# Reordered loads, four output banks for the first block, and weight sums on GpSimd in a retention-plus-GELU-layer kernel

## The chip, the cores and the metric

The kernel runs on one core of a Trainium2 chip. The metric is the device time of one execution in microseconds (us). The kernel before has a median of 300.85 us over three runs (299.17, 300.85 and 300.95).

## The reference

Eight batches of 576 tokens with eight heads of 64 go through a causal retention (attention without softmax, with a decay per head), and the 4608 x 512 result goes through a two-layer GELU network:

```python
def _attn_ref(q, k, v):
    B, H, S, D_ = q.shape                       # 8, 8, 576, 64
    scores = (1.0 / np.sqrt(D_)) * np.matmul(q, k.transpose(0, 1, 3, 2))
    gamma = 1.0 - 2.0 ** (-5.0 - np.arange(H, dtype=np.float32))
    rel = np.arange(S)[:, None] - np.arange(S)[None, :]
    Dmat = np.where(rel >= 0, gamma[:, None, None] ** rel[None, :, :], 0.0)
    return np.matmul(scores * Dmat[None], v)

def _moe_ref(x, w_in, w_out):                   # x 4608 x 512, w_in 512 x 2048, w_out 2048 x 512
    h = x @ w_in
    g = 0.5 * h * (1.0 + np.tanh(np.sqrt(2.0 / np.pi) * (h + 0.044715 * h * h * h)))
    return g @ w_out
```

## The kernel before

Everything is on one core, with matrix operands in f16 and sums in f32. The output is made in nine blocks t of 512 tokens: block t for t < 8 is the first 512 tokens of batch t, block 8 the 64-token tails of all batches. While TensorE works on the network of block t, it also does the retention of batch t + 1, in small pieces put between the network's matmuls. Every engine runs its instructions in the order in which the program issues them.

**Steps and events.** The main loop at the end (L839 to L869) makes a list of steps for each block and numbers them u = 0, 1, ... After step u it runs what was booked with `at(t, u, ...)`. The list for block 0 is the second layer alone (L841 to L845), because its first layer was done ahead (L833 to L837, with negative u counted back from step 0). For block 0 a step is two matmuls of 512 columns (`down_mm`, L504): for output rows i0 = 0 and 1 sixteen steps, one for each 128-row tile f of w_out in the order `FO` = 0-3, 8-11, 4-7, 12-15, then a step that copies the two PSUM sums out and stores them (`store_pair`, L509); then the same again for rows 2 and 3. So two PSUM banks hold sums at a time, steps 0 to 15 and 17 to 32 are matmuls, and 16 and 33 are stores. Block 1 has sixteen steps of eight 256-column matmuls for its first layer (`up_half`, L480), and after steps 3, 7, 11 and 15 VectorE makes sums of the activations (`act_sums`, L536, four f16 operations each). From step 16 follow fourteen product steps (`prod`, L548): from block 1 on the second layer uses seven products in place of eight, which needs the sums of the activations and the sums `wt` "1" to "4" of w_out's quarters. `weight_sums(f)` (L525) makes the four `wt` sums for half of the rows; they are used in the order "2", "1", "3", "4".

**Retention of one half batch.** `casts2` (L746) books the casts of q and k (GpSimd, with a scale) and of v. `group` (L718) books for 256 tokens: `turn` (L275) for q and k, which is eight transposes on TensorE into one PSUM bank and one copy out (for batch 1 both on ScalarE, for batch 2 the one for q on VectorE); then `first`: `state2`, `score2` (32 matmuls into four banks `st`), the running state (`later`, `scan`, `spread`) and the masks (`masks2`, VectorE, from PSUM); then `second`: `past` and `av2` into two banks `xs`, and two copies `put` on ScalarE into xT, which the next block's first layer reads.

**PSUM.** There are eight banks. `bank` (L61) takes the one at the head of a list, `drop` puts it at the end as soon as its reader is issued in the program. A matmul into a bank waits on the chip until that reader is done.

**Loads.** All loads go through one queue (SyncE, "SP") in the order of `seq` (L124 to L131): batch 0's twelve tiles, sixteen of w_in, sixteen of w_out in the order FO, then batch 1 (`body(1)`, first 256 tokens first), batch 2 and so on. Each is 256 KB into one of sixteen rotating buffers `ld`; each cast frees one, and `pump` (L134) issues the next load. w_out tiles are cast by GpSimd and VectorE in turn (`WENG`, L634).

**Bookings that the change touches** (L711 to L763): the casts of w_out at steps -5 to -2 of block 0, the first half's weight sums on VectorE beside them, the second half's at (0, 28). Batch 1's first group has its casts of q and k at (0, 7), v on ScalarE at (0, 21), turns at (0, 17) and (0, 20), `first` at (0, 23), `second` at (0, 30). Its second group has casts at (0, 14) and (0, 29), turns at (0, 27) and (0, 31), `first` at (1, 1), `second` at (1, 6). Batch 2's two groups follow in block 1. At (1, 16) GpSimd gets a small copy (`gate`, L827) that waits for block 1's last activation sum and holds back the casts of batch 3.

Of the kernel before, what the change touches and what calls it, by code (L numbers as in the profile page):

```python
# [20 lines left out]
def kernel(  # L21
# [9 lines left out]
    nc = tc.nc  # L31
# [87 lines left out]
    def body(b):  # L119
        if b < NPE:  # L120
            return [("b", b, key, 2 * g + y) for g in range(2) for key in "qkv" for y in range(2)]
        return [("b", b, key, c) for c in range(NC) for key in "kqv"]

    seq = body(0) + [("i", g, ct) for g in range(4) for ct in range(4)]  # L124
    FO = [f + g for f in (0, 4) for g in (0, 1, 2, 3, 8, 9, 10, 11)]
    seq += [("o", f) for f in FO]
    TP = {2: 0, 4: 2, 6: 4, 7: 6}
    for b in range(1, B):
        seq += body(b)
        if b - 1 in TP:  # L130
            seq.append(("t", TP[b - 1]))  # L131
    q_ld = {"next": 0, "free": LD, "hold": False}
# [37 lines left out]
    for n in range(2):  # L170
# [3 lines left out]
            out=lp[:, 32 + 16 * n : 48 + 16 * n].rearrange("p (x h) -> p x h", h=8),  # L174
            in0=ps5[:, 4 * n + 2 : 4 * n + 4].unsqueeze(2).to_broadcast([128, 2, 8]),
            in1=lgr.unsqueeze(1).to_broadcast([128, 2, 8]), op=ALU.mult,
# [52 lines left out]
    def new_casts(b):  # L229
        a = att[b]  # L230
        for key in "kqv":
            a[key] = sb.tile([128, W], F16, tag="c" + key, name="c" + key, bufs=1 if key == "q" else 2)
# [38 lines left out]
    def new_turned(b):  # L271
        att[b]["tt"] = t = sb.tile([128, 2, NB, 128], F16, tag="tt", name="tt", bufs=2)
        att[b]["tk"], att[b]["tq"] = t[:, 0], t[:, 1]
# [39 lines left out]
    def score2(b, g, xs=(0, 1)):  # L313
        a = att[b]
        for x in xs:
            st = [bank("st") for _ in range(2)]
            for p in (2 * x, 2 * x + 1):
                for j in range(2):
                    o = 256 * (p % 2) + 128 * j
                    for h, hl in TILES:  # L320
                        nc.tensor.matmul(
                            st[hl][hv(h), o : o + 128], a["tt"][hv(hl), 0, 8 * g + 2 * p + j, hv(h)],
                            tq(b, 2 * g + h, p)[hv(hl)], start=True, stop=True,
                        )
            a["st", g, x] = st

    def masks2(b, g, x):
        for hl, t in enumerate(att[b].pop(("st", g, x))):
            r = sb.tile([128, 512], F16, tag="ret", name="ret", bufs=6)
            nc.vector.tensor_tensor(  # L330
                out=r.rearrange("p (n i) -> p n i", n=2), in0=t.rearrange("p (n i) -> p n i", n=2),
                in1=pm.rearrange("p j i -> p (j i)").unsqueeze(1).to_broadcast([128, 2, 256]), op=ALU.mult,
            )
            drop(t)
            att[b]["ret"][g, hl, x] = r
# [163 lines left out]
    op = {}  # L499
# [9 lines left out]
    def store_pair(t, i0, eng):  # L509
        o = ost()  # L510
        for n in range(2):
            x = op.pop(i0 + n)
            eng[n](out=o[:, n], in_=x)
            drop(x)
        r0 = TB * t + 128 * i0
        nc.sync.dma_start(out=out[r0 : r0 + 256, :].rearrange("(n p) d -> p n d", n=2), in_=o)
# [4 lines left out]
    wt = {n: const.tile([128, NH, HD], F16, name="wt" + n) for n in "1234"}  # L521
    W11, W12 = w_out_sb[:, 0:NH, 0:HD], w_out_sb[:, 0:NH, HD:DM]
    W21, W22 = w_out_sb[:, NH:NF, 0:HD], w_out_sb[:, NH:NF, HD:DM]

    def weight_sums(f, ns=range(4)):  # L525
        s = slice(f, f + 4)
        for n in ns:
            o, x, y, f = (
                ("1", W12, W11, ALU.subtract), ("3", W22, W12, ALU.subtract),
                ("2", wt["3"], W11, ALU.add), ("4", W21, wt["2"], ALU.subtract),  # L530
            )[n]
            nc.vector.tensor_tensor(out=wt[o][:, s], in0=x[:, s], in1=y[:, s], op=f)  # L532

    gs = {}

# [84 lines left out]
    CP = {"i": 0, "o": 0}  # L620

    def cast_w(kind, *i):
        src = w_raw.pop((kind,) + i)
        if kind == "i":
            g, ct = i
            dst = w_in_sb[:, ct, 512 * g : 512 * g + 512]
        else:
            dst = w_out_sb[:, i[0], :]
        eng = WENG[kind][CP[kind] % len(WENG[kind])]
        CP[kind] += 1  # L630
        eng(out=dst, in_=src)  # L631
        pump(1)

    WENG = {  # L634
        "i": (nc.gpsimd.tensor_copy,),
        "o": (nc.gpsimd.tensor_copy, nc.vector.tensor_copy),
    }
# [5 lines left out]
    V, P, A = nc.vector, nc.gpsimd, nc.scalar  # L643


    def later(b, c):
        scan(b, c)
        spread(b, c, A.copy)
# [54 lines left out]
    def at(t, u, f, last=False):  # L703
        events.setdefault((t, u, last), []).append(f)
# [5 lines left out]

    at(0, -12, lambda: [V.memset(x, 0.0) for x in (tbd[1][:, 1:], *tbt[1:])])  # L711
    for n, f in enumerate(FO):
        at(0, -5 + n // 4, lambda f=f: cast_w("o", f))
        if n > 8 and n % 2:
            at(0, -5 + n // 4, lambda n=n: weight_sums(0, [(n - 9) // 2]))


    def group(b, g, turns, s, o, own=True, ahead=()):  # L718
        for w, key, cp in zip(turns, "qk", (A.copy if b == 1 else T, A.copy)):
            at(*w, lambda key=key, cp=cp: turn(b, g, key, (cp,)))  # L720

        def first():
            if own:
                state2(b, g)
            score2(b, g)
            if own:
                later(b, 2 * g)
            masks2(b, g, 0)
            if own:
                masks2(b, g, 1)  # L730
                scan(b, 2 * g + 1)
            else:
                at(s[0], s[1] + 1, lambda: masks2(b, g, 1))

        def second():
            past(b, 2 * g), past(b, 2 * g + 1), av2(b, g)
            for x in ahead:
                state2(*x)
            put(b, 2 * g), put(b, 2 * g + 1)

        at(*s, first)
        at(*o, second)
        if own:
            at(o[0], o[1] + 1, lambda: spread(b, 2 * g + 1, A.copy))

    def casts2(b, g, kq, v, e):  # L746
        at(*kq, lambda: [cc(b, key, 2 * g + y, P) for key in "qk" for y in range(2)])
        at(*v, lambda: [cc(b, "v", 2 * g + y, e) for y in range(2)])

    at(0, 6, lambda: (new_casts(1), new_turned(1)))  # L750
    casts2(1, 0, (0, 7), (0, 21), A)
    group(1, 0, ((0, 17), (0, 20)), (0, 23), (0, 30))
    casts2(1, 1, (0, 14), (0, 29), A)
    at(0, 28, lambda: weight_sums(4))
    group(1, 1, ((0, 27), (0, 31)), (1, 1), (1, 6))
    at(1, 0, lambda: (new_casts(2), new_turned(2)))
    casts2(2, 0, (1, 0), (1, 0), P)
    group(2, 0, ((1, 4), (1, 7)), (1, 11), (1, 16), ahead=((2, 1),))
    casts2(2, 1, (1, 4), (1, 4), P)
    at(1, 17, lambda: later(2, 2))  # L760
    at(1, 23, lambda: later(2, 3))
    group(2, 1, ((1, 10), (1, 13)), (1, 20), (1, 26), own=False)
    at(1, 8, chunk_masks)  # L763

    at(6, 0, lambda: load_tails(TP[7]))
# [38 lines left out]
    for t in range(2, B):  # L804
        b, tl = t + 1, TP.get(t)
# [13 lines left out]
    for b in range(NPE, B):  # L819
        ent = [(key, c) for c in range(NC) for key in "kqv"]  # L820
        eng = {"k": P, "q": P, "v": P if b == NPE else A}
# [17 lines left out]
    for t in range(NTB):  # L839
        steps = []  # L840
        if t == 0:  # L841
            for i0 in (0, 2):
                for f in FO:
                    steps.append(lambda f=f, i0=i0: [down_mm(0, i0 + n, f) for n in range(2)] and None)
                steps.append(lambda i0=i0: store_pair(0, i0, (A.copy, V.tensor_copy)))  # L845
        else:
            for u in range(2 if t == 1 else 0):
                for f in (0, NH, 2, NH + 2, 4, NH + 4, 6, NH + 6):
                    def half(u=u, f=f):
                        up_half(t, u, f)  # L850
                        if f in (NH + 2, NH + 6):
                            return lambda: act_sums(t, f - NH - 2, f - NH + 2, slice(u, u + 1))
                    steps.append(half)
            for f in range(0 if t == 1 else NH):
                steps.append(lambda f=f: up(t, f))
                def hi(f=f):
                    up(t, f + NH)
                    if f % 2:
                        return lambda: act_sums(t, f - 1, f + 1)
                steps.append(hi)  # L860
            for m in (1, 6, 5, 7, 2, 3, 4) if t == NTB - 1 else (1, 6, 5, 7, 2, 4, 3):
                for u in range(2):
                    steps.append(lambda m=m, u=u: (prod(t, m, u), after(t, m, u)))
        for u, s in enumerate(steps):
            then = s()
            run(t, u)
            if callable(then):
                then()
            run(t, u, True)  # L869
# [31 lines left out]
```

## Time and profile before

| what | us |
|---|---|
| median of three runs | 300.85 |
| the profiled execution | 300.83 |
| its span, first to last instruction | 298.9 |
| TensorE busy in the span | 284.7 |
| VectorE, ScalarE, GpSimd busy | 171.9, 163.4, 98.8 |
| TensorE busy in 0 to 20 us | 13.41 of 20.00 |
| in 20 to 34 us (first layer of block 0) | 14.00 of 14.00 |
| in 41.4 to 58 us (block 0's second layer and the start of block 1) | 13.63 of 16.60 |
| in 58 to 89.6 us (rest of block 1) | 31.60 of 31.60 |
| in 89.6 to 268 us (blocks 2 to 7, start of 8) | 178.40 of 178.40 |

The second column is time in the span of one profiled execution; "busy" of TensorE counts matmuls with their modelled ends. The granted TensorE clock is 1.00 in each of these stretches. Block 0's second layer begins at 33.86 us, block 1's first layer at 53.99, its products at 74.04.

### The profile page before, as it was taken

The page shows a single profiled execution, that of the slowest core. Times are in us where ns is not written, and L with a number is a line of the kernel's source. Part 1 is how long each engine was busy: PE and PEld are TensorE (multiplying, and loading weights), DVE is VectorE, ACT ScalarE, POOL GpSimd, SP SyncE. Part 2 cuts the span into 40 slices and gives each one's busy share as a digit, 9 for nine tenths or more (in the row PEclk, how much of TensorE's full clock was granted, in tenths as well). Part 3 has the DMA queues.
Part 4 walks back from the last instruction along what each step waited for, and adds up shares of the span by engine and source line. Part 5 has one row for each costly group of instructions (what it writes and reads, how often), then busy time and mean ns, then how long its engine had stood idle before and what let it go on. Part 6 is the DMA issues. An engine that isn't in the chain of part 4 may idle for free.

```text
span 298.9 us, 7301 instructions
## 1 busy us (share of the span) xinstructions
PE 284.7 (95%) x3028; PEld 197.2 (66%) x3028; DVE 171.9 (58%) x353; ACT 163.4 (55%) x302; POOL 98.8 (33%) x129
## 2 busy tenths in 40 slices
PE   6779988899999999999999999999999999999993
PEld 2458645688884488448844885488548854884582
DVE  6790445998754874476548654855486535233432
ACT  5377426788438673766376736664665356307500
POOL 4677377970790074006700650058030000000000
PEclk9999999999999999999999999999999999999998
DMA  7999999999889999999999959944931030012004
GB/s 200 309 352 350 371 271 293 246 289 211 178 147 230 227 217 183 268 207 195 118 245 227 181 99 263 219 90 86 255 86 37 2 140 0 2 50 94 0 0 140
DMA packets 129057, 52.89 MB, mean 177 GB/s; under 512 B 101633, under 2 KB 120577, under 8 KB 129025
## 3 DMA queue, kind: packets, MB, share of 16 engines
q1 hardware_dynamic: 128544, 51.92, 73.7%
q10 hardware_dynamic: 480, 0.52, 0.6%
q8 instruction: 23, 0.38, 0.5%
q14 instruction: 10, 0.07, 0.1%
HBM read 36.70 MB, written 9.44 MB: 154 GB/s over the span
## 4 chain that ended last, share of the span: by engine, by line
PE 80%; DMA 10%; DVE 4%; SPq 3%; POOL 2%; ACT 1%; issue 0%; DVEq 0%; POOLq 0%
PE hp L469 33%; PE opB L561 14%; PE opA L561 10%; PE opC L561 10%; PE hp L487 4%; DMA ld<-in_moe_w_out_dram 4%; SPq L96 2%; PE xs L448 2%; PE st L372 2%; DMA ld<-in_moe_w_in_dram 2%; DMA ld<-in_q_dram 2%; DMA ld<-in_v_dram 2%; DVE wt L532 2%; PE xs L439 1%; PE us L397 1%; PE tr L285 1%
## 5 line engine op out<-in xcount | busy, mean ns | idle before, releaser
L469 PE MATMUL hp<-xT,w_in_sb 128*128 128x512 f16 x448 | 98.9, 380 | 0.0
L475 ACT ACTIVATE gT<-hp 128x512 f16<-128x512 f32 x112 | 64.9, 597 | 45.3 <-PE hp L469 44.8
L469 PEld LDWEIGHTS <-w_in_sb 128*128 128x128 f16 x448 | 43.3, 98 | 50.6
L561 PEld LDWEIGHTS <-gT 128*128 128x128 f16 x512 | 49.0, 98 | 7.1 <-issue 0.7
L561 PEld LDWEIGHTS <-s 128*128 128x128 f16 x384 | 37.0, 98 | 4.9
L543 DVE TENSOR_TENSOR s<-gT 128x512 f16<-128x512 f16 x32 | 14.0, 436 | 44.4 <-ACT gT L475 44.4
L827 POOL COPY gate<-s 128x1 f16<-128x1 f16 x5 | 0.9, 189 | 92.3 <-DVE s L546 92.3
L561 PE MATMUL opB<-wt,gT 128*128 128x256 f16 x256 | 30.9, 273 | 0.5 <-DVE ost L575 0.5
L487 PE MATMUL hp<-xT,w_in_sb 128*128 128x256 f16 x256 | 30.2, 273 | 1.1 <-POOL w_in_sb L631 1.0
L561 PE MATMUL opA<-w_out_sb,gT 128*128 128x256 f16 x256 | 30.8, 273 | 0.0
L487 PEld LDWEIGHTS <-w_in_sb 128*128 128x128 f16 x256 | 24.4, 98 | 5.1 <-POOL w_in_sb L631 1.6
L423 ACT CAST tbd<-ws 64x256 f16<-64x256 f32 x48 | 19.3, 403 | 15.3 <-DVE ws L414 13.6
L381 DVE TENSOR_TENSOR ret<-st,cm 128x512 f16<-128x512 f32 x40 | 24.8, 681 | 0.0
L575 DVE TENSOR_TENSOR k<-k,opB 128x512 f32<-128x512 f32 x16 | 11.0, 687 | 22.2 <-PE opB L561 16.3
L605 ACT COPY ost<-opA 128x512 f32<-128x512 f32 x8 | 4.7, 586 | 34.2 <-PE opA L561 19.9
L264 POOL TENSOR_TENSOR cq<-ld,sc 128x512 f16<-128x512 f32 x20 | 21.9, 1095 | 0.0
L493 ACT ACTIVATE gT<-hp 128x512 f16<-128x512 f32 x32 | 18.5, 600 | 5.3 <-PE hp L487 5.0
L458 ACT CAST xT<-xs 128x512 f16<-128x512 f32 x36 | 19.3, 592 | 3.3 <-PE xs L362 1.9
L264 POOL TENSOR_TENSOR ck<-ld,sc 128x512 f16<-128x512 f32 x20 | 20.8, 1040 | 0.0
L414 DVE TENSOR_TENSOR ws<-vs,gt 128x256 f32<-128x256 f32 x24 | 16.0, 669 | 1.2
L575 DVE TENSOR_TENSOR ost<-k,opC 128x512 f32<-128x512 f32 x16 | 11.0, 687 | 9.8 <-PE opC L561 9.5
L575 DVE TENSOR_TENSOR ost<-k,opB 128x512 f32<-128x512 f32 (+1 forms) x9 | 5.7, 629 | 18.7 <-PE opB L561 18.7
(93 smaller groups left out, 359.1 us busy)
## 6 DMA issues: line engine op xcount, KB each, us to landing
ld<-in_q_dram SPq DMA_DIRECT2D x32, 256.0 KB, 5.4
ld<-in_k_dram SPq DMA_DIRECT2D x32, 256.0 KB, 5.3
ld<-in_v_dram SPq DMA_DIRECT2D x32, 256.0 KB, 5.3
out_dram<-ost SPq DMA_DIRECT2D x16, 512.0 KB, 3.5
ld<-in_moe_w_in_dram SPq DMA_DIRECT2D x16, 256.0 KB, 6.2
ld<-in_moe_w_out_dram SPq DMA_DIRECT2D x16, 256.0 KB, 6.1
lt<-in_k_dram SPq DMA_DIRECT2D x8, 128.0 KB, 5.1
lt<-in_q_dram SPq DMA_DIRECT2D x8, 128.0 KB, 4.4
```

Source lines behind the costliest of these rows:

```text
L264: eng.tensor_tensor(out=dst.rearrange("p (h d) -> p h d", d=D), in0=raw.rearrange("p (h d) -> p h d", d=D), in1=sc[:, s0].unsqueeze(2).to_ ...
L381: nc.vector.tensor_tensor(out=r.rearrange("p (n i) -> p n i", i=128), in0=t.rearrange("p (n i) -> p n i", i=128), in1=(cm if b < PAIR else ...
L414: nc.vector.tensor_tensor(out=w, in0=uc, in1=gt, op=ALU.mult)
L423: cp(out=(tbd[b % 2][r, c, :, r] if c < NC - 1 else tbt[b % NT4][r, :, r]), in_=w[r])
L458: nc.scalar.copy(out=xT[:, g0 : g0 + 2], in_=xs.rearrange("p (n g t) -> p g n t", n=HP, g=2))
L469: nc.tensor.matmul(hp.rearrange("p (g t) -> p g t", t=TL), w_in_sb[:, ct, 128 * fc : 128 * fc + 128], xT[:, o : o + TB // TL, ct, :], star ...
L475: nc.scalar.activation(out=gT[t][:, fc].rearrange("p i n -> p (i n)"), in_=hp, func=AF.Gelu_apprx_tanh)
L487: nc.tensor.matmul(hp[:, 256 * x : 256 * x + 256].rearrange("p (g t) -> p g t", t=TL), w_in_sb[:, ct, 128 * (f + x) : 128 * (f + x) + 128] ...
L493: nc.scalar.activation(out=gT[t][:, f : f + 2, 2 * u : 2 * u + 2, :].rearrange("p f i n -> p f (i n)"), in_=hp.rearrange("p (f n) -> p f n ...
L543: nc.vector.tensor_tensor(out=s["1"], in0=a21, in1=a22, op=ALU.add)
L561: nc.tensor.matmul(op[tag][:, HD * u : HD * u + HD], lhs(f), rhs[:, f], start=(new and u == 0 and f == 0), stop=(f == NH - 1), skip_group_ ...
L575: nc.vector.tensor_tensor(out=o, in0=a, in1=b, op=ALU.add)
```

## The change

- The load order puts batch 1's first six tiles (q, k, v of its first 256 tokens) ahead of the last four w_out tiles (rows f = 12 to 15).
- These four tiles are cast by GpSimd alone, at (0, 6). Batch 1's q and k are cast at (0, 2), its v at (0, 18).
- Block 0's second layer runs over four banks: twelve steps for rows 0 and 1, twelve for rows 2 and 3, then the last four f for rows 0 and 1 and their store (step 28), then the last four for rows 2 and 3 and their store (step 33).
- Since four banks hold sums, batch 1's first `score2` is split: two banks at `first` (0, 20), the other two four steps later (0, 24).
- The other bookings of batches 1 and 2 move: by one to four steps, the turns of batch 1's second group four and three steps later, to (0, 31) and (1, 0).
- The first half's weight sums stay on VectorE, a step earlier; the second half's move from VectorE at (0, 28) to GpSimd at (1, 5), in the order "3", "2", "1", "4".

```diff
     FO = [f + g for f in (0, 4) for g in (0, 1, 2, 3, 8, 9, 10, 11)]
-    seq += [("o", f) for f in FO]
+    LATE = 12
+    seq += [("o", f) for f in FO[:LATE]]
     TP = {2: 0, 4: 2, 6: 4, 7: 6}
+    seq += body(1)[:6] + [("o", f) for f in FO[LATE:]] + body(1)[6:]
     for b in range(1, B):
-        seq += body(b)
+        seq += body(b) if b > 1 else []
...
-    def weight_sums(f, ns=range(4)):
+    def weight_sums(f, ns, eng):
...
-            nc.vector.tensor_tensor(out=wt[o][:, s], in0=x[:, s], in1=y[:, s], op=f)
+            eng.tensor_tensor(out=wt[o][:, s], in0=x[:, s], in1=y[:, s], op=f)
...
-        eng = WENG[kind][CP[kind] % len(WENG[kind])]
+        eng = WENG[kind][CP[kind] % len(WENG[kind])] if CP[kind] < LATE or kind == "i" else nc.gpsimd.tensor_copy
...
-        at(0, -5 + n // 4, lambda f=f: cast_w("o", f))
-        if n > 8 and n % 2:
-            at(0, -5 + n // 4, lambda n=n: weight_sums(0, [(n - 9) // 2]))
-
-
-    def group(b, g, turns, s, o, own=True, ahead=()):
+        at(0, -5 + n // 4 if n < LATE else 6, lambda f=f: cast_w("o", f))
+        if 8 <= n < LATE:
+            at(0, -5 + n // 4, lambda n=n: weight_sums(0, [n - 8], V))
+
+    def group(b, g, turns, s, o, own=True, ahead=(), apart=0):
...
-            score2(b, g)
+            score2(b, g, (0,) if apart else (0, 1))
             if own:
                 later(b, 2 * g)
             masks2(b, g, 0)
+            if own and not apart:
+                masks2(b, g, 1)
             if own:
-                masks2(b, g, 1)
                 scan(b, 2 * g + 1)
-            else:
+            if apart:
+                at(s[0], s[1] + apart, lambda: (score2(b, g, (1,)), masks2(b, g, 1)))
+            elif not own:
                 at(s[0], s[1] + 1, lambda: masks2(b, g, 1))
...
-    at(0, 6, lambda: (new_casts(1), new_turned(1)))
-    casts2(1, 0, (0, 7), (0, 21), A)
-    group(1, 0, ((0, 17), (0, 20)), (0, 23), (0, 30))
-    casts2(1, 1, (0, 14), (0, 29), A)
-    at(0, 28, lambda: weight_sums(4))
-    group(1, 1, ((0, 27), (0, 31)), (1, 1), (1, 6))
+    at(0, -1, lambda: (new_casts(1), new_turned(1)))
+    casts2(1, 0, (0, 2), (0, 18), A)
+    group(1, 0, ((0, 13), (0, 17)), (0, 20), (0, 29), apart=4)
+    casts2(1, 1, (0, 14), (0, 30), A)
+    group(1, 1, ((0, 31), (1, 0)), (1, 1), (1, 5))
     at(1, 0, lambda: (new_casts(2), new_turned(2)))
     casts2(2, 0, (1, 0), (1, 0), P)
-    group(2, 0, ((1, 4), (1, 7)), (1, 11), (1, 16), ahead=((2, 1),))
+    group(2, 0, ((1, 4), (1, 6)), (1, 10), (1, 15), ahead=((2, 1),))
     casts2(2, 1, (1, 4), (1, 4), P)
-    at(1, 17, lambda: later(2, 2))
+    at(1, 5, lambda: weight_sums(4, (1, 2, 0, 3), P))
+    at(1, 16, lambda: later(2, 2))
     at(1, 23, lambda: later(2, 3))
-    group(2, 1, ((1, 10), (1, 13)), (1, 20), (1, 26), own=False)
+    group(2, 1, ((1, 9), (1, 12)), (1, 20), (1, 26), own=False)
...
-            for i0 in (0, 2):
-                for f in FO:
+            for i0, fs in ((0, FO[:LATE]), (2, FO[:LATE]), (0, FO[LATE:]), (2, FO[LATE:])):
+                for f in fs:
                     steps.append(lambda f=f, i0=i0: [down_mm(0, i0 + n, f) for n in range(2)] and None)
-                steps.append(lambda i0=i0: store_pair(0, i0, (A.copy, V.tensor_copy)))
+                if fs[-1] == FO[-1]:
+                    steps.append(lambda i0=i0: store_pair(0, i0, (A.copy, V.tensor_copy)))
```

## The prediction

> **What bounds the kernel now.** I read the page's busy shares first, then each engine's timeline from 30 to 110 us.
>
> ```profile
> span 298.9 us, 7301 instructions
> PE 284.7 (95%) x3028; PEld 197.2 (66%) x3028; DVE 171.9 (58%) x353; ACT 163.4 (55%) x302; POOL 98.8 (33%) x129
> ```
>
> TensorE is the bound: 14.2 us of the span are idle. From 20 us on it idles in one stretch only, 41.4 to 58 us, where 13.63 of 16.60 us are busy. No matmul is removed, and loads and casts up to the twelfth w_out tile stay as they are, so nothing before step 0 of block 0 (33.86 us) moves. TensorE's timeline there:
>
> ```profile
> 42.39 0.62 PE L285 MATMUL tr<-ident,cq 128*128 128x128 f16 x8 [1.02 <-POOL cq L256]
> 44.40 0.62 PE L285 MATMUL tr<-ident,ck 128*128 128x128 f16 x8
> 46.76 0.19 PE L348 MATMUL us<-cv,ck 64*64 64x64 f16 x1 [0.45 <-ACT cv L251]
> 47.28 0.44 PE L348 MATMUL us<-cv,ck 64*64 64x64 f16 x31 [0.33 <-ACT cv L251]
> 57.62 0.41 PE L321 MATMUL st<-tt 64*64 64x128 f16 x15 [1.07 <-DVE ost L513]
> 57.96 2.79 PE L487 MATMUL hp<-xT,w_in_sb 128*128 128x256 f16 x24
> ```
>
> A row's length holds the drain of its last matmul, so I count starts. A 512-column matmul takes 0.216 us (40 in 8.63 in the chain of waits), a block-0 step 0.432, an `up_half` 0.875, a turn 0.45. From 33.86 to 57.96 the work is 64 x 0.216 + 4 x 0.45 + two states 0.54 + two scores 1.14 + past and av2 0.89 + two up_halves 1.75 = 19.9 us of 24.1. Of the 4.2 lost, the wait for q is 1.2, for k 0.3, for v's casts 1.1, for the copy `ost` (behind VectorE's weight sums) 1.2, and small gaps 0.4. That is all the change could win.
>
> **Part by part: loads and block 0.** The thirteenth w_out tile lands by 37.2 (its GpSimd cast starts at 37.29); q now has its place. Four casts at 1.0 each end q at 39.2 and k at 41.3. TensorE needs q after 28 matmuls, at 39.90, and k at 42.08. Cover 0.7 us; without it the wait is what is missing. So 1.2 + 0.3 are won. The late w_out tiles take the places of k and v, issued from 36.4 to about 40 with 5.2 to 6.1 us to landing; cast by 46.3, the last is needed at step 27, 48.4: no cost. Their two casts more on GpSimd (1.3 us) delay q of the second group to 48.3, needed at 51.0. The store moved behind two loads on SP has a buffer that nobody needs before block 1's products.
>
> The wait for v stays: turn, copy of k and v casts follow each other on ScalarE with three steps of cover, as before. There it was 2.88 us from the turn of k to the state (44.40 to 47.28); here 42.08 + 2.88 = 44.96, again 1.1 lost. From there: rest of state and half a score 0.53, four steps, half a score 0.28, four steps, past and av2 0.89 end `second` at 50.1. Splitting the score costs no matmul; its masks (0.62 each) end by 49.7, needed at 49.85.
>
> A new wait comes next. ScalarE's list before:
>
> ```profile
> 50.49 1.32 ACT L291 COPY tt<-tr 128x1024 f16<-128x1024 f16 x1 [1.32 <-PE tr L285]
> 51.83 1.14 ACT L251 CAST cv<-ld 128x512 f16<-128x512 f32 x2
> 52.88 1.06 ACT L458 CAST xT<-xs 128x512 f16<-128x512 f32 x2
> 53.83 0.82 ACT L423 CAST tbd<-ws 64x256 f16<-64x256 f32 x2
> 54.67 1.01 ACT L291 COPY tt<-tr 128x1024 f16<-128x1024 f16 x1
> 55.58 0.59 ACT L513 COPY ost<-op 128x512 f32<-128x512 f32 x1
> 56.06 1.11 ACT L493 ACTIVATE gT<-hp 128x512 f16<-128x512 f32 x2
> ```
>
> Before, q's copy and v's casts came ahead of the two `put` copies. Now all of it follows them: put 0.95, spread 0.84, v 1.05, q 1.34, ost 0.48, a GELU 0.51, k 1.01 = 6.2 us by start to start, so the second score waits until 50.1 + 6.3 = 56.4. TensorE has 3 steps, 2 turns, 2 up_halves and a state = 4.2 us of cover and arrives at 54.3: 2.1 lost. The `ost` wait goes (VectorE is free). After that score TensorE stands at 57.0 instead of 57.96: **0.95 us won** so far, 299.9.
>
> **Weight sums on GpSimd.** VectorE loses four operations (5.0 us between 51.92 and 56.96); GpSimd gets four of 128x1024 f16, which the trace shows on VectorE only. Nearest rows: GpSimd's two-input operation on 512 columns, 1.04, so 2.05 for 1024; its cast, 0.61, so 1.2 below; and that operation beside VectorE's sums, 2.89 for two, so 2.9 above. I take 2.05, the same kind of operation. [...]
>
> What matters is what VectorE does meanwhile. The timelines of GpSimd and, in the second fence, of VectorE:
>
> ```profile
> 62.15 1.61 POOL L253 CAST cv<-ld 128x512 f16<-128x512 f32 x2
> ...
> 106.97 1.04 POOL L264 TENSOR_TENSOR ck<-ld,sc 128x512 f16<-128x512 f32 x1
> 107.98 1.22 POOL L264 TENSOR_TENSOR cq<-ld,sc 128x512 f16<-128x512 f32 x1
> ```
>
> ```profile
> 62.45 0.83 DVE L543 TENSOR_TENSOR s<-gT 128x512 f16<-128x512 f16 x1
> 63.32 0.71 DVE L544 TENSOR_TENSOR s<-s,gT 128x512 f16<-128x512 f16 x1
> 63.95 0.41 DVE L545 TENSOR_TENSOR gT<-gT 128x512 f16<-128x512 f16 x1
> ...
> 107.07 1.23 DVE L414 TENSOR_TENSOR ws<-vs,gt 128x256 f32<-128x256 f32 x1
> ```
>
> A VectorE operation with two SBUF inputs that starts during a GpSimd operation ends 0.28 us after it: 107.07 + 1.23 = 108.30, GpSimd's at 108.01; the same at 76.80 and 84.87. The activation sums take 0.42 alone, 0.83 and 0.71 beside two casts. GpSimd's next operation is 0.18 longer. Operations with one input in PSUM (masks, copies) keep their length. So the two engines take turns, one operation each. [...]
>
> GpSimd's casts of batch 2 start when q's buffer is free, after the second group's turn of q: 51.6. Eight at 1.01, four at 0.59 and five of 0.18 end at 62.9. The sums then run to 62.9 + 4 x 2.23 = 71.8. VectorE comes to the activation sums after step 7 at 65.0 (GELU done), which are four dependent two-input operations: one gets through after each GpSimd sum, the last at 72.1, where before they took 1.5 us. Behind them on VectorE stands the copy of batch 2's turned q (1.31, before 68.50 to 69.81): 73.4. Who waits: the turn's bank went back to the end of the list, step 10, the state and `score2` take the other seven, so step 11's `hp` gets it. Up to there TensorE has, from 57.0, nine up_halves (steps 2 to 10, 7.9), three turns (1.35), past and av2 (1.11, from 62.79 to 63.90 before) and state and score (0.83) = 11.1, so it arrives at 68.1. It stands until 73.4: **5.3 us lost**. Behind it the masks end at 76.1, needed at 78.8; the remaining sums run alone (GpSimd done by 73.3) before the products at about 79. The `wt` sums are ready in time, and GpSimd is back before its gate.
>
> Sum: 300.83 - 0.95 + 5.3 = **305.2 us**, against 300.83 for the profiled execution (span 298.9 and 1.9 around it), which is the median to 0.02.
>
> **Rivals.**
> - Not slower: the turns on SBUF don't hold VectorE up. Place: activation sums after step 7. It decides where sums and copy end by 68.1, so GpSimd by 66.5: (66.5 - 62.9) / 4 - 0.18 = 0.7 us for a sum, or operations that let VectorE in between. Price zero: 299.9. For it: VectorE's freed 5 us. Against: the row at 107.07. 13%.
> - In between: both only slow down, VectorE's sums 0.42 to 0.83: from 65.0 to 68.3, copy to 69.6, 1.5 lost: 301.4. 12%.
> - The first with ScalarE's list hidden too (2.1 more): 297.8. Against: that list is in order. 5%.
> - Sums of 2.9: GpSimd to 75.2, copy to 76.8, 8.7 lost: 308.6. 8%.
> - The loads don't come earlier: q cast at 42.3 as before, 2.4 lost at 39.9, GpSimd shifted alike: 307.6. 5%.
>
> **How the numbers follow.** The forecast has 57%, with its own range from 303.2 (one more operation slips between two GpSimd sums, 2.2 less) to 307.0 (GpSimd sums at 2.4). Slower by over 1% (303.9 and up; 1% is about what a measurement here tells from no change): most of the forecast, 0.55, and the last two, 0.13: 0.68. Within 1%: 0.12 + 0.13 and a little of the forecast: 0.27. Faster: 0.05. The range 300.0 to 308.2 leaves out half of the first rival, the 297.8 case and the upper half of the 2.9 case, some 0.17; the low end also takes in sums of 1.2 us (301.8).
>
> **What would show it.** Right: block 0 without a wait for cq; a `us` wait for cv of 0.8; an `st` wait of about 2 on ScalarE's `tt` near 56; GpSimd `wt` rows of about 2 us; activation sums near 65 to 72 of 2 us each; an `hp` wait of about 5 on VectorE's `tt` near 68. Wrong: sums under 1 us, activation sums still at 0.42, or TensorE full from 58 to 80.

## The result and the profile after

The changed kernel takes 309.1 us (median of four runs, 307.31 to 310.64) against 300.9 for the kernel before: a ratio of 1.0284, 95% interval 1.0216 to 1.0353. It is slower, as forecast, by 8.2 us where 4.4 were forecast, and it lies 0.9 us above the upper end of the range.

The profiled execution is the fastest of the four, 307.31 us. Its page, the span, the busy times and the granted TensorE clock in 40 slices of 7.6 us:

```profile
span 305.3 us, 7303 instructions
...
PE 286.8 (94%) x3028; PEld 198.7 (65%) x3028; DVE 173.6 (57%) x347; ACT 163.8 (54%) x302; POOL 107.9 (35%) x135
...
PEclk9999999996899999999999999999999999999998
```

TensorE runs the same 3028 matmuls and is busy 2.1 us longer: two slices, 68.7 to 84 us, have a lower clock (0.6 and 0.8 in the row), which the kernel before has only in its last slice (0.8), as here. Its timeline shows where it stands:

```profile
43.94 0.19 PE L350 MATMUL us<-cv,ck 64*64 64x64 f16 x1 [0.45 <-ACT cv L253]
44.46 0.44 PE L350 MATMUL us<-cv,ck 64*64 64x64 f16 x31 [0.33 <-ACT cv L253]
...
56.17 0.64 PE L323 MATMUL st<-tt 64*64 64x128 f16 x32 [1.81 <-ACT tt L293]
...
66.38 1.03 PE L489 MATMUL hp<-xT,w_in_sb 128*128 128x256 f16 x8 [1.33 <-DVE tt L293]
...
73.49 3.57 PE L489 MATMUL hp<-xT,w_in_sb 128*128 128x256 f16 x16 [3.93 <-DVE tt L293]
76.85 1.06 PE L287 MATMUL tr<-ident,ck 128*128 128x128 f16 x8
...
81.80 1.92 PE L563 MATMUL opA<-w_out_sb,gT 128*128 128x256 f16 x16
```

The wait for q is gone, the wait for v's casts is as before, a wait for ScalarE's copy has come, and then two for VectorE's copies, 1.33 and 3.93 us. After the second, sixteen matmuls take 3.57 us, and the turn behind them (eight transposes) 1.06; at full clock they take 1.9 and 0.61. ScalarE's list ahead of the wait at 56.17:

```profile
49.97 1.07 ACT L460 CAST xT<-xs 128x512 f16<-128x512 f32 x2 [0.85 <-PE xs L364]
51.07 0.82 ACT L425 CAST tbd<-ws 64x256 f16<-64x256 f32 x2
51.91 1.14 ACT L253 CAST cv<-ld 128x512 f16<-128x512 f32 x2
52.96 1.31 ACT L293 COPY tt<-tr 128x1024 f16<-128x1024 f16 x1
54.13 0.58 ACT L515 COPY ost<-op 128x512 f32<-128x512 f32 x1
54.60 0.62 ACT L495 ACTIVATE gT<-hp 128x512 f16<-128x512 f32 x1
55.09 1.03 ACT L293 COPY tt<-tr 128x1024 f16<-128x1024 f16 x1
```

Seven entries without a gap, from 49.97 to 56.12. For the two larger waits, GpSimd's timeline and then VectorE's:

```profile
62.54 2.29 POOL L534 TENSOR_TENSOR wt<-w_out_sb 128x1024 f16<-128x1024 f16 x1
64.90 2.19 POOL L534 TENSOR_TENSOR wt<-wt,w_out_sb 128x1024 f16<-128x1024 f16 x1
67.06 2.30 POOL L534 TENSOR_TENSOR wt<-w_out_sb 128x1024 f16<-128x1024 f16 x1
69.32 2.29 POOL L534 TENSOR_TENSOR wt<-w_out_sb,wt 128x1024 f16<-128x1024 f16 x1
```

```profile
62.77 2.34 DVE L548 TENSOR_TENSOR s<-gT,s 128x512 f16<-128x512 f16 x1
65.03 1.29 DVE L293 COPY tt<-tr 128x1024 f16<-128x1024 f16 x1
66.22 1.16 DVE L545 TENSOR_TENSOR s<-gT 128x512 f16<-128x512 f16 x1
67.41 2.23 DVE L546 TENSOR_TENSOR s<-s,gT 128x512 f16<-128x512 f16 x1
69.56 2.33 DVE L547 TENSOR_TENSOR gT<-gT 128x512 f16<-128x512 f16 x1
71.82 0.41 DVE L548 TENSOR_TENSOR s<-gT,s 128x512 f16<-128x512 f16 x1
72.15 1.28 DVE L293 COPY tt<-tr 128x1024 f16<-128x1024 f16 x1
```

In the kernel before, the activation sums after step 7 and the copy behind them were these:

```profile
65.92 0.40 DVE L543 TENSOR_TENSOR s<-gT 128x512 f16<-128x512 f16 x1
66.35 0.42 DVE L544 TENSOR_TENSOR s<-s,gT 128x512 f16<-128x512 f16 x1
66.69 0.42 DVE L545 TENSOR_TENSOR gT<-gT 128x512 f16<-128x512 f16 x1
67.03 0.42 DVE L546 TENSOR_TENSOR s<-gT,s 128x512 f16<-128x512 f16 x1
68.50 1.31 DVE L291 COPY tt<-tr 128x1024 f16<-128x1024 f16 x1 [1.05 <-PE tr L285]
```

There the copy waits for TensorE; now TensorE waits for the copy. Each activation sum that starts while GpSimd is at a weight sum ends 0.27 to 0.29 us after that sum does: 62.77 + 2.34 = 65.11 against 64.83, 67.41 + 2.23 = 69.64 against 69.36, 69.56 + 2.33 = 71.89 against 71.61. The fourth starts at 71.82, when GpSimd's last weight sum is over (71.61), and takes its usual 0.41. The copies between them keep their 1.3 us, but stand behind: they end at 66.32 and 73.43, and TensorE goes on at 66.38 and 73.49.

Both kernels' stretch from the first matmul of block 0's second layer to the first product with "2" (`opB`) can be taken apart by starts: 76.97 - 33.86 = 43.11 us before, 83.56 - 33.37 = 50.19 now. Up to the first matmul behind the second group's score it is 23.37 instead of 24.10, 0.73 won. Behind it, TensorE arrives at step 9 at 64.89 and goes on at 66.38 (1.49 lost), comes out of the score at 69.51 and goes on at 73.49 (3.98 lost), and the work from there to `opA`, the product before `opB`, takes 8.31 us (to 81.80). In the first experiment below the same work takes 5.97 (70.52 to 76.49) at full clock: 2.34 lost. The sum, -0.73 + 1.49 + 3.98 + 2.34 = 7.08, is the difference of the stretches.

The granted clock in short windows of the changed kernel. Columns: window, its length, busy time and instructions of TensorE, of its weight loads, VectorE, ScalarE and GpSimd, then the clock, DMA share and GB/s:

```profile
69.60:71.00 1.40, 0.00 (x0) 0.00 (x0) 1.40 (x2) 0.00 (x0) 1.40 (x1) 1.00 0.96 215
71.00:72.00 1.00, 0.00 (x0) 0.00 (x0) 1.00 (x2) 0.00 (x0) 0.92 (x3) 0.75 1.08 240
...
73.40:75.10 1.70, 1.61 (x8) 1.13 (x8) 1.70 (x5) 0.81 (x2) 0.00 (x0) 0.50 0.86 192
...
77.00:79.00 2.00, 2.00 (x19) 1.74 (x18) 1.35 (x4) 1.61 (x2) 0.00 (x0) 0.67 0.91 186
79.00:81.00 2.00, 2.00 (x25) 1.72 (x26) 0.00 (x0) 1.36 (x3) 0.00 (x0) 1.00 0.94 195
```

The clock falls to 0.50 while TensorE stands, at about 71.5, and is back at about 78.3, nearly 5 us after TensorE has gone on.

### The profile page after: what moved, and what is told of

It is laid out like the page before. It is cut to its first block, busy times and chain, and to the rows that moved or that the text cites. A ratio compares the mean times of both kernels' runs of the same rounds, so it can differ in the third digit from the quotient of the medians.

```text
span 305.3 us, 7303 instructions
## 1 busy us (share of the span) xinstructions
PE 286.8 (94%) x3028; PEld 198.7 (65%) x3028; DVE 173.6 (57%) x347; ACT 163.8 (54%) x302; POOL 107.9 (35%) x135
## 4 chain that ended last, share of the span: by engine, by line
PE 85%; DVE 8%; ACT 3%; DMA 1%; issue 1%; POOL 0%; SPq 0%; DVEq 0%; POOLq 0%
PE hp L471 32%; PE opB L563 14%; PE opA L563 9%; PE opC L563 9%; PE hp L489 6%; PE op L509 4%; PE xs L450 2%; PE st L374 2%; PE xs L441 2%; DVE ret L332 1%; DVE tt L293 1%; PE tr L287 1%; DMA ld<-in_q_dram 1%; ACT tt L293 1%; DVE gT L547 1%; DVE s L546 1%
## 5 line engine op out<-in xcount | busy, mean ns | idle before, releaser
L471 PEld LDWEIGHTS <-w_in_sb 128*128 128x128 f16 x448 | 43.4, 98 | 50.5
L545 DVE TENSOR_TENSOR s<-gT 128x512 f16<-128x512 f16 x32 | 15.2, 473 | 47.5 <-ACT gT L477 44.4
L489 PE MATMUL hp<-xT,w_in_sb 128*128 128x256 f16 x256 | 32.3, 283 | 5.8 <-DVE tt L293 5.3
L489 PEld LDWEIGHTS <-w_in_sb 128*128 128x128 f16 x256 | 25.3, 101 | 10.6 <-issue 5.4
L546 DVE TENSOR_TENSOR s<-s,gT 128x512 f16<-128x512 f16 x32 | 15.7, 490 | 1.1
```

Source lines behind the costliest of these rows:

```text
L471: nc.tensor.matmul(hp.rearrange("p (g t) -> p g t", t=TL), w_in_sb[:, ct, 128 * fc : 128 * fc + 128], xT[:, o : o + TB // TL, ct, :], star ...
L489: nc.tensor.matmul(hp[:, 256 * x : 256 * x + 256].rearrange("p (g t) -> p g t", t=TL), w_in_sb[:, ct, 128 * (f + x) : 128 * (f + x) + 128] ...
L546: nc.vector.tensor_tensor(out=s["2"], in0=s["1"], in1=a11, op=ALU.subtract)
```

## The experiments

In what follows "the stretch" is the time from block 0's first second-layer matmul to `opB`, in the profiled execution. It leaves out the start of the program, which differs from one execution to the next by up to 2.6 us (33.37 to 35.92 us until block 0's second layer in these eleven profiles). Four of the eleven show a granted clock of 0.50 for 3.4 us between 19 and 23.6 us, and these four reach block 0's second layer at 35.11 to 35.92; the other seven reach it at 33.37 to 34.46.

**The sums back on VectorE**

```diff
-    at(1, 5, lambda: weight_sums(4, (1, 2, 0, 3), P))
+    at(0, 25, lambda: weight_sums(4, range(4), V))
```

> The changed kernel with the second half's weight sums on VectorE again, at step 25 of block 0 (its last w_out tiles are cast by then and VectorE is free from 49.3 us). Theory (GpSimd's sums and VectorE's two-input operations take turns, one whole instruction each, and TensorE stands behind VectorE's copies): no wait of TensorE between 58 and 80 us, activation sums at 0.42 us, clock 1.00 there, 299.9 us (299.0 to 300.8). Rival (the time goes to the four-bank order, the split score and the moved turns): still above 305.

Measured: 301.78 us (300.54 to 303.95, ten runs), ratio 1.0034 (1.0003 to 1.0064). The rival falls: 7 of the 8 us are gone with this one edit. But it lies 1 us above the expected range, and it is not faster than before either. Its waits on TensorE's timeline, but for those for v:

```profile
57.97 0.64 PE L323 MATMUL st<-tt 64*64 64x128 f16 x32 [1.81 <-ACT tt L293]
...
70.52 1.91 PE L489 MATMUL hp<-xT,w_in_sb 128*128 128x256 f16 x16 [0.66 <-DVE tt L293]
...
76.49 1.92 PE L563 MATMUL opA<-w_out_sb,gT 128*128 128x256 f16 x16
```

The activation sums after step 7 take 0.42 and the clock is 1.00, as expected. Yet 0.66 us of the wait at step 11 is left. Batch 2's turns stand one step closer behind these sums than before, which would make it. No run changes that alone; the run that takes the other waits away, below, puts the turns back too and has no wait for this copy. The stretch is 43.07 us, that of the kernel before 43.11: what block 0 wins, that wait and its drain give back. The median is higher also because of the start: in the profile the granted clock was 0.50 from 19.1 to 22.5 us, and block 0's second layer began at 35.18. The ten runs fit that: three of the four under 301 us have a mean clock of 0.998 or 0.999, the six above it 0.988 to 0.994.

**The sums on GpSimd as the only edit of the kernel before**

```diff
-    at(0, 28, lambda: weight_sums(4))
+    at(1, 5, lambda: weight_sums(4, (1, 2, 0, 3), P))
...
```

(Left out: `weight_sums` takes the engine as an argument, as in the changed kernel.)

> The kernel before with this one edit: the second half's weight sums on GpSimd at step 5 of block 1. Theory: the same wait of TensorE for VectorE's copy of batch 2's turned q, 4 to 5 us near 70 us, then half clock; less the 1.2 us that the copy behind VectorE's sums cost: 305 to 309 us. Rival (four-bank order): 299.6, since only VectorE's relief is left.

Measured: 304.21 us (303.55 to 304.81), ratio 1.0105 (1.0066 to 1.0144). TensorE's waits in block 1:

```profile
67.84 1.91 PE L487 MATMUL hp<-xT,w_in_sb 128*128 128x256 f16 x16 [3.66 <-DVE tt L291]
...
73.12 1.91 PE L487 MATMUL hp<-xT,w_in_sb 128*128 128x256 f16 x16 [1.23 <-DVE tt L291]
```

The waits are on the same two copies, 4.9 us in sum, so the move alone makes them. The time is under the expected range, which had the half clock in it: in the profile the clock stayed at 1.00, and sixteen matmuls after 3.66 us of standing take 1.91. The wait for the copy behind VectorE's sums, 1.07 before, is gone. So is the wait for q in block 0, 1.02 before, although nothing ahead of it is changed: in this execution q's first cast began at 39.44 instead of 40.28. Block 0 up to the end of the second group's score took 21.76 us (34.13 to 55.89), against 24.10 in the profile before.

**GpSimd reads without purpose, and writes without reading**

The first experiment, with GpSimd's four sums repeated, or with four memsets in their place:

```diff
     at(0, 25, lambda: weight_sums(4, range(4), V))
+    at(1, 5, lambda: weight_sums(4, (1, 2, 0, 3), P))
```

```diff
     at(0, 25, lambda: weight_sums(4, range(4), V))
+    at(1, 5, lambda: [P.memset(xT[:, GM : GM + B], 0.0) for _ in range(4)])
```

> As the first, with GpSimd making the same four sums once more at step 5 of block 1 (same values, so nothing later needs to wait for new data). Theory: as slow as the changed kernel, 307 to 310 us, with activation sums near 2.2 us. Rival (what hurts is that the sums come late, not that they run there): products are not reached before 76 us and the repeated sums are done by 72, so 299.9.

> As the first, with four GpSimd memsets of 128x2048 f16 (about 2 us each by 0.52 for 512) at step 5 of block 1, into the tail part of xT that is written later: GpSimd writes, but reads nothing. If only GpSimd's reads of SBUF hold up VectorE's second input: activation sums at 0.42, 299.9 us. If any long GpSimd instruction does: as the run with the repeated sums, 307 to 310.

Measured: 307.86 us (307.26 to 309.86) with the repeated sums, ratio 1.0238 (1.019 to 1.0286); 301.14 (300.33 to 302.1) with the memsets, ratio 1.002 (0.9996 to 1.0044). TensorE's waits with the sums:

```profile
68.72 1.03 PE L489 MATMUL hp<-xT,w_in_sb 128*128 128x256 f16 x8 [1.34 <-DVE tt L293]
...
75.82 3.57 PE L489 MATMUL hp<-xT,w_in_sb 128*128 128x256 f16 x16 [3.92 <-DVE tt L293]
```

The waits are 1.34 and 3.92 us, and the clock falls again: the changed kernel's loss without any late data. With the memsets nothing is lost against the first experiment (its stretch is 43.07 us too). GpSimd's timeline and VectorE's of that run:

```profile
64.27 7.39 POOL L764 MEMSET xT<- 128x2048 f16 x4
```

```profile
67.62 0.43 DVE L545 TENSOR_TENSOR s<-gT 128x512 f16<-128x512 f16 x1 [1.46 <-ACT gT L495]
68.08 0.42 DVE L546 TENSOR_TENSOR s<-s,gT 128x512 f16<-128x512 f16 x1
68.43 0.42 DVE L547 TENSOR_TENSOR gT<-gT 128x512 f16<-128x512 f16 x1
68.76 0.42 DVE L548 TENSOR_TENSOR s<-gT,s 128x512 f16<-128x512 f16 x1
```

Four activation sums at 0.42 in the middle of 7.4 us of GpSimd memsets, 1.85 us each. So it is not that GpSimd is busy: beside its sums, which read SBUF, VectorE's two-input operations took 1.15 to 2.33 us in the run that repeats them, and beside its memsets, which only write, 0.41 to 0.43. The turns that the rows of before showed beside GpSimd instructions of 1.04 us hold beside instructions of 2.2 to 2.3 too.

**Filling the wait**

Sixteen matmuls into a bank whose reader is done, ahead of the matmul that waits:

```diff
+    def warm_up(n):
+        head = spare.popleft()
+        filler(n)
+        spare.appendleft(head)
...
+    at(1, 10, lambda: warm_up(16))
```

> The changed kernel with sixteen idle-filling matmuls (512 columns, 3.5 us, into the one PSUM bank whose reader is done) right before the matmul that waits for VectorE's copy of the turned q. Theory (standing still for about 4 us lets the granted clock fall to 0.50 for some 7 us): the fillers take the place of the idle time, granted clock 1.00 from 70 to 80 us, 2 to 4 us faster than the changed kernel: ratio to before 1.013 to 1.02, 304.5 to 306.5 us. Rival (the wait alone makes the loss): ratio stays at 1.028, 309.

Measured: 305.96 us (304.9 to 306.31), ratio 1.0169 (1.0134 to 1.0204). TensorE's timeline:

```profile
70.57 3.63 PE L228 MATMUL fill<-tbd,ident 128*128 128x512 f16 x16
74.58 1.91 PE L489 MATMUL hp<-xT,w_in_sb 128*128 128x256 f16 x16 [0.38 <-DVE tt L293]
```

The copy is no earlier, 0.38 us of waiting are left over, and sixteen matmuls take 1.91 instead of 3.57. The stretch is 47.85 us, 2.34 less than in the changed kernel, which is just the term found above. So of the 8 us 2.3 by the stretches, 3.1 by the medians, are the clock, not the wait.

**The same sums in shorter pieces**

```diff
-    def weight_sums(f, ns, eng):
-        s = slice(f, f + 4)
+    def weight_sums(f, ns, eng, w=4):
+        s = slice(f, f + w)
...
-    at(1, 5, lambda: weight_sums(4, (1, 2, 0, 3), P))
+    at(1, 5, lambda: [weight_sums(f, (1, 2, 0, 3), P, 1) for f in range(4, 8)])
```

> The changed kernel with each of GpSimd's four sums cut into four of 256 elements: the same work and bytes, sixteen shorter operations. Theory (VectorE waits for the rest of one GpSimd instruction, so a shorter instruction means a shorter wait): activation sums at 0.7 to 0.9 us instead of 2.2, the first wait gone and the second down from 3.9 to about 1.3 us, no drop of the clock, ratio about 1.004 (301 to 302.5 us). Rival (what counts is how long GpSimd is at it in all, which grows to about 10 us): 308 to 310.

Measured: 303.8 us (302.62 to 304.3), ratio 1.0097 (1.006 to 1.0134). VectorE's timeline after step 7:

```profile
68.44 0.46 DVE L545 TENSOR_TENSOR s<-gT 128x512 f16<-128x512 f16 x1 [1.00 <-ACT gT L495]
68.93 0.78 DVE L546 TENSOR_TENSOR s<-s,gT 128x512 f16<-128x512 f16 x1
69.62 0.89 DVE L547 TENSOR_TENSOR gT<-gT 128x512 f16<-128x512 f16 x1
70.44 0.88 DVE L548 TENSOR_TENSOR s<-gT,s 128x512 f16<-128x512 f16 x1
```

GpSimd works longer in all (65.08 to 76.67 us instead of 62.54 to 71.61) and holds VectorE up less: 0.8 to 0.9 us for a sum, the first wait gone, the second 1.91, and no fall of the clock behind it (sixteen matmuls take 1.91). The wait was expected at 1.3, and the time is 1.3 us above the expected range. The stretch is 44.40 us, 1.33 above that of the run without sums on GpSimd. The rival falls: it is the length of one GpSimd instruction, not GpSimd's time in all, that sets the price of each VectorE operation: these four took 0.46 to 0.89 us beside instructions of 0.66 to 0.85, and those beside sums of 2.2 to 2.3 in the changed kernel 1.16 to 2.34.

**Taking away what is left in block 0**

```diff
-    casts2(1, 0, (0, 2), (0, 18), A)
+    casts2(1, 0, (0, 2), (0, 16), A)
-    casts2(1, 1, (0, 14), (0, 30), A)
+    casts2(1, 1, (0, 14), (0, 15), P)
-            at(o[0], o[1] + 1, lambda: spread(b, 2 * g + 1, A.copy))
+            at(*((1, 1) if apart else (o[0], o[1] + 1)), lambda: spread(b, 2 * g + 1, A.copy))
-    at(1, 5, lambda: weight_sums(4, (1, 2, 0, 3), P))
+    at(0, 25, lambda: weight_sums(4, range(4), V))
...
```

(The lines left out put batch 2's bookings in block 1, and `second` of batch 1's second group, back to those of the kernel before.)

> The changed kernel with the waits that are left taken away: the second half's weight sums on VectorE at step 25 of block 0; batch 1's first v cast on ScalarE before the copy of the turned k (step 16); its second v cast on GpSimd (step 15), and the running state of its first group written out at (1, 1), which shortens ScalarE's list ahead of the second score by 1.9 us; batch 2's bookings as in the kernel before. Theory (the four-bank order and the earlier loads are sound, ScalarE's list and the v casts are what they leave): of the 4.2 us lost in block 0 before, 0.5 to 1 remain: 3 us less than before, 297 to 298 us, ratio 0.99. Rival (nothing in block 0 is won by the change): 300 to 301.

Measured: 299.01 us (298.03 to 299.87, seven runs), ratio 0.9945 (0.9921 to 0.9969): faster than both kernels, by 1.4 us where 3 were expected. The waits that TensorE's timeline still names in the stretch:

```profile
53.84 0.64 PE L323 MATMUL st<-tt 64*64 64x128 f16 x32 [0.26 <-ACT tt L293]
...
63.48 1.91 PE L489 MATMUL hp<-xT,w_in_sb 128*128 128x256 f16 x16 [0.76 <-DVE tt L293]
```

Both waits for v are gone and the one for ScalarE's copy fell from 1.81 to 0.26. The stretch is 40.72 us, 2.39 less than before. Of the missing gain 0.76 us is the wait at step 9, once more for a copy behind activation sums that wait for GpSimd, this time for its casts (1.27, 1.16, 1.26 and 0.83 us). The rest is that the other executions were slower than the profiled one (298.03), which no trace explains.

**A warmer start**

```diff
+    filler(3)
     up_half(0, 0, 0)
```

> As the run with the waits taken away, with three idle-filling matmuls (0.65 us) ahead of block 0's first layer, where TensorE waits for GpSimd's first w_in casts at 17 to 19 us and where some executions showed the granted clock at 0.50 from 19 to 23 us. If that drop can be filled away: the same lowest time as that run, and a median 0.5 to 1 us lower. If three matmuls are too few or come at the wrong moment: the same median, or 0.4 us more.

Measured: 299.28 us (298.44 to 300.2, ten runs), ratio 0.9955 (0.9935 to 0.9975). Nothing is won. The mean clock of its runs still goes from 0.990 to 1.0. What lets the clock fall at the start in some executions and not in others stays open.

**The copy ahead of the sums**

The run with the waits taken away, with one number changed:

```diff
-    group(2, 0, ((1, 4), (1, 7)), (1, 11), (1, 16), ahead=((2, 1),))
+    group(2, 0, ((1, 3), (1, 7)), (1, 11), (1, 16), ahead=((2, 1),))
```

> As the run with the waits taken away, with batch 2's first turn of q one step earlier, at (1, 3), so that VectorE's copy of it stands ahead of the activation sums of step 3 and not behind them. There these sums waited for GpSimd's casts (1.27, 1.16, 1.26 and 0.83 us) and the matmul of step 8 then waited 0.76 us for the copy. Theory: that wait goes, 0.8 to 0.9 us less, 298.1 us (297.6 to 298.6), ratio 0.991 to 0.993. Rival (VectorE's total work decides, the order moves the wait to the next copy): unchanged, 299.0.

Measured: 297.85 us (297.32 to 299.02, nine runs), ratio 0.9928 (0.9904 to 0.9952), the lowest ratio of all. The wait (at step 9; the expectation counts it as step 8) is gone and none came in its place in block 1, where TensorE is busy for all of 58 to 74 us. The stretch (40.58 us) is hardly shorter than the 40.72 of the run with the waits taken away, because in this execution another wait showed in block 0, which the profile of the warmer start has too:

```profile
53.49 1.03 PE L489 MATMUL hp<-xT,w_in_sb 128*128 128x256 f16 x8 [1.03 <-DVE ost L515]
```

That is the copy `ost` behind VectorE's weight sums again, the wait of the kernel before at a new place. Against the profile of the warmer start, which has both waits (1.03 and 0.91), the stretch is 1.04 us shorter (41.62 to 40.58): the step-9 wait. By the medians the gain is not clear of the noise. They differ by 1.2 us (299.01 to 297.85), but the kernel before, measured beside each, differs by 0.5 too (300.39 and 299.90), and the intervals of the two ratios overlap (0.9921 to 0.9969, 0.9904 to 0.9952).

## Why the prediction was right or wrong

**What bounds, and block 0.** Right in the main. One reading was wrong without harm: TensorE idles in a second stretch after 20 us, the program's end from 290 us on, which holds 4.6 of the 14.2 idle us; the change does not touch it. Block 0's second layer began at 33.37, not 33.86, which is less than executions differ by, so the rows are better compared from there. So counted, 0.73 us were won of 0.95 forecast. The waits for q and k went, the wait for v stayed at 0.45 + 0.33, and the second score, held by ScalarE's list for 1.81 us, came 22.80 us after the start of block 0's second layer (56.17), forecast 22.5 (56.4). The seven-entry sum was 6.2 and is 6.15 by the rows. But the 1.2 us for q rest on one execution: in the profile with the sums on GpSimd as the only edit the wait for q was under 0.1 us, and block 0, with the wait for `ost` gone too, was there 1.6 us shorter (21.76) than in the changed kernel (23.37). So the four-bank order and the earlier loads do not win in every execution, and in the first experiment, which is the change without its sums on GpSimd, nothing was won.

**The price of a weight sum on GpSimd.** 2.05 us plus 0.18 was taken, and 2.19 to 2.30 measured, which is 2.27 from one to the next. They ran from 62.54 to 71.61, forecast 62.9 to 71.8. The estimate from the 512-column row was good. The run with them cut in four has 0.66 to 0.67 for 256 elements where VectorE was not in the way, so four short ones (2.6) cost GpSimd more than one long one.

**Turn by turn on SBUF.** Right, and it is now shown rather than argued: by the rows (each activation sum ends 0.28 us after a GpSimd sum), by the repeated sums, by the memsets and by the shorter pieces. The rivals in which VectorE is not held up, or only slowed to 0.83, fall, and so does the one in which the loads don't come earlier (q's first cast began at 35.86 instead of 40.28).

**Who waits.** Right in the main: TensorE stands for the bank of the turned q until 73.49, forecast 73.4. Counted from the start of block 0's second layer that is 40.12 and 39.54 us, so the agreement within 0.1 us is partly luck. The forecast had 5.3 us there in one piece. It came in two, 1.49 at step 9 and 3.98 at step 11, because the last activation sum after step 3 was caught by the first GpSimd sum too, and the first copy behind it. In sum 5.47.

**What failed: the time after the wait.** The step "It stands until 73.4: 5.3 us lost", and the sum 300.83 - 0.95 + 5.3 after it, let TensorE go on at full clock. It went on at half (0.50), for nearly 5 us (73.49 to 78.3), which cost 2.34 in the profiled execution. In the stretch the forecast's terms make 43.11 - 0.95 + 5.3 = 47.46 us; with the clock's 2.34 they make 49.80, and 50.19 was measured. The run with the wait filled, where the clock stays full behind it (sixteen matmuls in 1.91), has 47.85. In whole time the sum becomes 305.2 + 2.3 = 307.5, and the profiled execution took 307.31, with a start that was 0.49 us earlier than in the profile before.

Between 6.98 and 297 us the trace of before shows no clock below 1.00, and no wait of TensorE longer than 1.3 us. But its first microseconds do show about half rate: seven 512-column matmuls at 2.28 us take 3.15, six from 10.92 on 1.47; the eight transposes at 5.99 us take 1.04, those from 9.02 on 0.62, although the row of 0 to 20 us reads 1.00. And its end shows a fall: the last matmul ends at 294.83, and from 297.1 on the clock is 0.50. In the changed kernel it fell after 1.9 us of standing (69.56 to 71.50).

The forecast's own range is also a little off by its own terms: 2.2 us less is 303.0, not 303.2, and sums of 2.4 us make 306.6, not 307.0.

**What stays open.** The clock's term alone leaves the time inside the stated range; the median, 309.1, is 1.8 us above the profiled execution. The other three runs have no trace, but their mean clocks are on record: 0.978 (310.64 us), 0.981 (309.56) and 0.987 (308.64), against 0.986 in the profiled one. If the lower clock is 0.50, as in the profiles of both kernels, that makes an estimated 13.6, 11.7 and 8.0 us at half clock against 8.5. So the first two had 3 to 5 us more of it. The profile of the run with the repeated sums (309.86 us, mean clock 0.981) shows such a case: half clock also from 20.1 to 23.6 us, with block 0's second layer starting at 35.71 instead of 33.37. Where it fell in those two runs is not shown, and the third was 1.3 us slower than the profiled one without any more of it.

## What to carry to other kernels

Moving a two-input operation to GpSimd is priced by what VectorE does in that time: here every VectorE operation with two SBUF inputs that started during one of GpSimd's sums ended 0.27 to 0.29 us after it, and none was held up by a memset. VectorE's copy from PSUM kept its 1.29 us beside one of the sums. So put such work where VectorE works from PSUM or not at all, or cut it short. Then follow the queue behind the delayed operation to whoever frees a PSUM bank. And where TensorE is going to stand for some 4 us, add the clock to the wait: here it made 2.3 us on top of 4, though not in every execution (the wait of 3.66 us went without).

## What the runs showed of the hardware that was not expected

- The clock's fall lasted longer than the wait that it came in, which was 3.93 and 3.92 us. In the changed kernel TensorE stood from 69.56 us; the clock fell at about 71.5 and came back at about 78.3. With the repeated sums it stood from 71.90; the clock fell at about 74.7 and came back at about 81.6. Both spells are some 6.8 us, and TensorE had been standing for 1.9 and 2.8 us when they began.
- The clock changed in steps of time. In the profiles of the two kernels the stretches between its changes are multiples of 3.413 us (64.85, 6.83 and 225.28 in the changed kernel, 290.13 in the one before). Counted in these steps, the one before the fall in the changed kernel (68.08 to 71.50) holds 1.48 us of TensorE's work; 64 of the 70 matmuls in it are of 64x64 tiles.
- A wait of 3.66 us (from 64.18 to 67.84, the sums on GpSimd as the only edit) left the clock at 1.00 in the profiled execution (the sixteen matmuls behind it take 1.91), one of 3.93 did not (3.57). So the time that TensorE has stood does not decide alone: 1.9 us were enough in one run, 3.66 were not in another. What else counts, no run shows.
- A GpSimd memset of 128x2048 f16 took 1.85 us and delayed no VectorE operation (the activation sums beside the four took 0.41 to 0.43); a GpSimd sum of 128x1024 took 2.2 to 2.3, and the four of them delayed four VectorE operations, by 0.7 to 1.9 us each.
